# Deep cross network, last layer: the first half of the batch computed in the transposed form

## The chip, the cores and the metric

The kernel runs on one core of one Trainium2 chip. Its time is the device time of one execution in microseconds; where several runs were made, their median is given. A profile is one execution taken by the hardware profiler. TensorE is called PE, VectorE DVE, ScalarE ACT, GpSimd POOL, and SP is the engine whose queue issues most of the DMAs.

## The reference

Six cross layers over a batch of 4096 rows with 416 features, in bf16. Each layer multiplies the running value by a 416 x 416 matrix, adds a bias, multiplies by the input elementwise and adds the running value:

```python
B, F, D, L = 4096, 26, 16, 6
Din = min(F * D, 1024)          # 416

def reference(x0, ws, bs):
    x = x0
    for l in range(ws.shape[0]):
        x = x0 * (x @ ws[l] + bs[l]) + x
    return x
```

## The kernel before

**Two forms.** In the transposed form features lie on the partitions and batch rows along the free dimension. The 416 features are three blocks of 128 (`XM[..]`, index `m` or `k`) and a remainder of 32. The batch is two halves `s` of 2048 rows, each of four groups `g` of 512; the remainders of the four groups of a half are stacked on the 128 partitions of `XR`. Layers one to five (indices 0 to 4) are computed in this form. In the row form batch rows lie on the partitions, 128 at a time, and the 416 features along the free dimension; the sixth layer (index 5, `LL`) is computed in this form, so that its result can be stored to the output as it stands.

**Layers two to five** (loop at line 282). For each tile `(s, m)`, PE runs `mm_full` (line 181: per group twelve matmuls, whose weights are 32 columns wide, four of them side by side) and `mm_row` (line 187: the 32 remainder features, four groups side by side) into two PSUM tiles of 128 x 1024. `ew_main` then takes each of the two: ACT evicts it with the bias (line 165), DVE multiplies by the input (166) and adds the running value (169). `rem_pair` computes the 32 remainder outputs of both halves of the batch (`mm_rem`, lines 193 and 198; `ew_rem`, lines 173 to 175). In the order of the code each tile's elementwise work follows its matmuls, and the two tiles of a turn are interleaved.

**What the row form needs.** Besides the weights, it needs the input in rows (`X0rows`, loaded by four DMAs at line 125) and the fifth layer's result in rows (`XLrows`). The latter comes from DMA transposes on the SP queue: while layer five runs (`feeds_last`), `xl_dmat` (line 205) transposes each finished tile of 128 features x 2048 rows into `XLrows`, and the remainder goes through `scrR` (line 274) and an ACT copy `xl_rem` (line 278).

**Layer six** (from line 315). A quad is four row tiles of 128 rows that share one block of the stacked remainders; there are eight, four in each half of the batch. `mm_q_full` (line 327) is three matmuls over 416 columns per row tile; `mm_q_rem` adds the remainder features (333) and the bias (336) of four row tiles. Quads are done in rounds of two that fill the four PSUM tiles; `PAIRS`, `TURNS` and `ENDS` say which PSUM place each row tile has, and whether two are evicted together. `ew` evicts one or two row tiles by ACT (354), multiplies by `X0rows` on DVE (355), and leaves the add of `XLrows` (344) and the store (345) to `close_sum` of the next call, so that an add runs behind the next product. All stores are issued on the SP queue but the last, which is on ACT's.

**What sets the order.** The code is written for a framework that finds the waits between engines. Each engine and each DMA queue executes in one order, which follows the order of the code; `keep_in_program_order` fixes it for an instruction. PSUM has four tiles of two banks (`bufs=4`, tag `ps`) for all of this; row results lie in ten buffers `o`.

Of the kernel before, what the change touches and what calls it, by code (L numbers as in the profile page):

```python
# [10 lines left out]
ALU = mybir.AluOpType  # L11
BF16 = mybir.dt.bfloat16
FP32 = mybir.dt.float32
# [3 lines left out]
def kernel(  # L17
# [7 lines left out]
    nc = tc.nc  # L25
    B, D = x0.shape
    L = ws.shape[0]
    P = 128
# [3 lines left out]
    NS = 2  # L32
    NG = 4
    CW = 512
    SW = NG * CW
    NBT = B // P
# [3 lines left out]
    big = ctx.enter_context(tc.tile_pool(name="big", bufs=1))  # L40
    tpool = ctx.enter_context(tc.tile_pool(name="tpool", bufs=6))
    opool = ctx.enter_context(tc.tile_pool(name="opool", bufs=10))
    psum = ctx.enter_context(tc.tile_pool(name="psum", bufs=4, space=bass.MemoryType.PSUM))

    x0_v = x0.rearrange("(bt p) d -> p bt d", p=P)
    out_v = out.rearrange("(bt p) d -> p bt d", p=P)
# [9 lines left out]
    bLr = const.tile([P, D], BF16)  # L56
    bM = const.tile([P, NK, L], FP32)
    bR = const.tile([P, L], FP32)
    X0rows = big.tile([P, NBT, D], BF16)
    XLrows = big.tile([P, NBT, D], BF16)  # L60
    scrR = [big.tile([P, 4, P], BF16, name=f"scrR{s}") for s in range(NS)]
    xrem = big.tile([P, 16, R], BF16)
# [2 lines left out]
    XM = [big.tile([P, NK, B], BF16, name=f"XM{i}") for i in range(3)]  # L65
    XR = [big.tile([P, NS * CW], BF16, name=f"XR{i}") for i in range(3)]

    def col0(s, g):
        return SW * s + CW * g

    def load_wm(eng, l):
        eng.dma_start(WM[:, l], ws[l, 0:NK * P, :].rearrange("(k p) n -> p k n", p=P))
# [48 lines left out]
        load_wr(nc.sync, g, 1, L)  # L121
    for l in range(2, L):
        load_wm(nc.sync, l)
    for q in range(4):
        nc.sync.dma_start(X0rows[:, 8 * q:8 * q + 8, :], x0_v[:, 8 * q:8 * q + 8, :])
    for g in range(NG):
        nc.sync.dma_start(bLr[32 * g:32 * g + 1, :], bs[LL:LL + 1, :])

# [33 lines left out]
    def ew_main(l, s, m, h, pt, cur, nxt, pin=False):  # L162
        c0 = col0(s, 2 * h)
        t = tpool.tile([P, 2 * CW], BF16, name="t")
        nc.scalar.activation(t[:], pt[:].rearrange("p a b -> p (a b)"), ACT.Identity, bias=bM[:, m, l:l + 1], scale=1.0)  # L165
        prod = nc.vector.tensor_tensor(out=t[:], in0=t[:], in1=XM[0][:, m, c0:c0 + 2 * CW], op=ALU.mult)  # L166
        if pin:
            tc.keep_in_program_order(prod)
        nc.vector.tensor_tensor(out=nxt[:, m, c0:c0 + 2 * CW], in0=t[:], in1=cur[:, m, c0:c0 + 2 * CW], op=ALU.add)  # L169
# [7 lines left out]
    def mm_full(l, s, m, g, pts, cur, first, last):  # L177
        c0 = col0(s, g)
        for k in range(NK):
            for q in range(4):  # L180
                nc.tensor.matmul(pts[g // 2][32 * q:32 * q + 32, g % 2, :], lhsT=WM[:, l, k, 128 * m + 32 * q:128 * m + 32 * q + 32],  # L181
                                 rhs=cur[:, k, c0:c0 + CW], start=(first and k == 0), stop=(last and k == NK - 1),
                                 tile_position=(0, 32 * q))

    def mm_row(l, s, m, pts, curR, first, last):
        for g in range(NG):
            nc.tensor.matmul(pts[g // 2][:, g % 2, :], lhsT=WR[32 * g:32 * g + 32, l, 128 * m:128 * m + 128],  # L187
                             rhs=curR[32 * g:32 * g + 32, CW * s:CW * s + CW],
                             start=first, stop=last, tile_position=(32 * g, 0))
# [11 lines left out]
    def new_pts():  # L201
        return [psum.tile([P, 2, CW], FP32, tag="ps", name=f"pt{h}") for h in range(2)]

    def xl_dmat(s, k, nxt):
        nc.sync.dma_start_transpose(out=XLrows[:, 16 * s:16 * s + 16, 128 * k:128 * k + 128],
                                    in_=nxt[:, k, SW * s:SW * s + SW])
# [57 lines left out]
    for s in range(NS):  # L264
        first_layer(s)

    def rem_pair(l, cur, curR, nxtR, feeds_last):
        pr2 = psum.tile([P, 2, CW], FP32, tag="ps", name="pr2")
        for s in range(NS):
            mm_rem(l, s, pr2[:, s, :], cur, curR)  # L270
        for s in range(NS):
            ew_rem(l, s, pr2[:, s, :], curR, nxtR)
            if feeds_last:
                nc.sync.dma_start_transpose(out=scrR[s][:], in_=nxtR[:, CW * s:CW * s + CW])

    def xl_rem(s):
        tc.keep_in_program_order(
            nc.scalar.copy(XLrows[:, 16 * s:16 * s + 16, NK * P:D].rearrange("p (g i) r -> p i g r", g=NG),
                           scrR[s][:].rearrange("p i (g r) -> p i g r", g=NG)))

    cur, curR = XM[1], XR[1]
    for l in range(1, LL):
        nxt, nxtR = XM[1 + (l % 2)], XR[1 + (l % 2)]
        feeds_last = (l == LL - 1)
        tiles = [(s, m) for s in range(NS) for m in range(NK)]
        pts = {}

        def finish(t):
            s, m = t
            for h in range(2):  # L290
                ew_main(l, s, m, h, pts[t][h], cur, nxt)
            if feeds_last:
                xl_dmat(s, m, nxt)

        for n in range(0, len(tiles), 2):
            ta, tb = tiles[n], tiles[n + 1]
            pts[ta] = new_pts()
            for g in range(NG):
                mm_full(l, ta[0], ta[1], g, pts[ta], cur, True, False)
            mm_row(l, ta[0], ta[1], pts[ta], curR, False, True)  # L300
            pts[tb] = new_pts()
            mm_row(l, tb[0], tb[1], pts[tb], curR, True, False)
            if feeds_last and n == 4:
                xl_rem(0)
            finish(ta)
            for g in range(NG):
                mm_full(l, tb[0], tb[1], g, pts[tb], cur, False, True)
            finish(tb)
            if n == 0:
                rem_pair(l, cur, curR, nxtR, feeds_last)  # L310
        if feeds_last:
            xl_rem(1)
        cur, curR = nxt, nxtR

    l = LL
    quads = [(s, i) for s in range(NS) for i in range(4)]
    NQ = len(quads)
    KD = NK * P

    def q_cols(q, g):  # L320
        s, i = quads[q]
        c = col0(s, g) + 128 * i
        return slice(c, c + 128)

    def mm_q_full(q, g, py, closes):
        for k in range(NK):
            nc.tensor.matmul(py[:, 0:D], lhsT=cur[:, k, q_cols(q, g)], rhs=WM[:, l, k, :],  # L327
                             start=((not closes) and k == 0), stop=(closes and k == NK - 1))

    def mm_q_rem(q, py, done):  # L330
        s, i = quads[q]
        for g in range(NG):
            nc.tensor.matmul(py[g][:, 0:D], lhsT=curR[32 * g:32 * g + 32, CW * s + 128 * i:CW * s + 128 * i + 128],  # L333
                             rhs=WR[32 * g:32 * g + 32, l, :], start=(g >= done), stop=False, tile_position=(32 * g, 0))
        for g in range(NG):
            nc.tensor.matmul(py[g][:, 0:D], lhsT=ones[32 * g:32 * g + 1, :],  # L336
                             rhs=bLr[32 * g:32 * g + 1, :], start=False, stop=(g < done), tile_position=(32 * g, 0))
# [9 lines left out]
    def ew(q, g0, n, src, eng):  # L347
        s, i = quads[q]
        b0 = 16 * s + 4 * g0 + i
        b = slice(b0, b0 + 4 * (n - 1) + 1, 4)  # L350
        t = tpool.tile([P, 2 * CW], BF16, name="t")
        o = opool.tile([P, 2, D], BF16, name="o")
        tv = t[:, 0:n * D].rearrange("p (a d) -> p a d", a=n)
        nc.scalar.copy(tv, src)  # L354
        tc.keep_in_program_order(nc.vector.tensor_tensor(out=tv, in0=tv, in1=X0rows[:, b, :], op=ALU.mult))  # L355
        close_sum()
        pending.append((o[:, 0:n, :], tv, XLrows[:, b, :], out_v[:, b, :], eng))

    PAIRS = [(0, 0), (0, 1), (1, 0), (1, 1), (2, 0), (2, 1), (3, 0), (3, 1)]
    TURNS = [(0, 0), (0, 1), (1, 0), (2, 0), (3, 0), (1, 1), (2, 1), (3, 1)]  # L360
    ENDS = [(0, 0), (1, 0), (2, 0), (0, 1), (3, 0), (1, 1), (2, 1), (3, 1)]
    rounds = [(0, PAIRS, 2), (2, PAIRS, 2), (4, TURNS, 2), (6, ENDS, 1)]
    for q, at, done in rounds:
        tiles = [psum.tile([P, 2, CW], FP32, tag="ps", name=f"py{n}") for n in range(4)]
        bank = [tiles[n][:, a, :] for n, a in at]

        def close(u, n):
            tl, a = at[u]
            ew(q + u // 4, u % 4, n, tiles[tl][:, a:a + n, 0:D], nc.scalar if q + 2 == NQ and u == 7 else nc.sync)

        for u in range(done):
            mm_q_full(q, u, bank[u], False)
        mm_q_rem(q, bank[0:4], done)
        close(0, done)
        mm_q_rem(q + 1, bank[4:8], 0)
        for u in range(done, 8):
            mm_q_full(q + u // 4, u % 4, bank[u], True)
            if at is not PAIRS:
                close(u, 1)
            elif u % 2:  # L380
                close(u - 1, 2)
    close_sum()


# [28 lines left out]
```

## Time and profile before

| quantity | value |
| --- | --- |
| time, median of 3 runs | 130.92 us (130.61 to 130.94) |
| span of the profiled execution | 128.9 us |
| time of the profiled execution beside its span | not given by the page |
| PE busy | 123.1 us (96%) |
| DVE busy | 107.1 us (83%) |
| ACT busy | 86.9 us (67%) |
| granted PE clock, mean | 0.998 |
| moved by DMA | 16.37 MB; HBM read 6.15 MB, written 3.41 MB |
| last layer on PE | 103.85 to 124.55 us |
| last DVE add ends | 126.32 us |

The span runs from the first to the last instruction of the profiled execution. Busy time is the time in which an engine had an instruction in work. In the page, a line such as `L181 PE MATMUL pt<-XM,WM` is a group of instructions of line 181 that read `XM` and `WM` and write `pt`; a chain is the work that ended last, followed back from the end; a timeline lists instructions by start and duration; a windows view gives busy times and the DMA traffic of chosen stretches.

### The profile page before, as it was taken

How to read it: one execution, taken by the hardware profiler on the slowest of the kernel's cores; microseconds unless marked ns; L12 is line 12 of the kernel's file. 1: busy time of each engine (PE TensorE's matmuls, PEld its weight loads, DVE VectorE, ACT ScalarE, POOL GpSimd, SP SyncE). 2: the span in 40 equal slices, each digit the busy share in tenths (PEclk: the TensorE clock that was granted, in tenths of full speed). 3: DMA queues.
4: the chain of work that ended last, by engine and by line, in shares of the span. 5: the costliest groups of instructions: out<-in, count | busy, mean ns of one | idle time of the engine just before them, and what ended most of it. 6: DMA issues, size and time to landing. Idle time of an engine off the chain costs nothing.

```text
span 128.9 us, 3973 instructions
## 1 busy us (share of the span) xinstructions
PE 123.1 (96%) x1690; PEld 54.9 (43%) x1690; DVE 107.1 (83%) x197; ACT 86.9 (67%) x99; POOL 5.9 (5%) x18
## 2 busy tenths in 40 slices
PE   6999999999999999999999999999999999999960
PEld 2343443354444444444444444444444445445420
DVE  1032979999999898989898989898989899898991
ACT  0426783987848577848668848668847896569670
POOL 4022200600000000000000000000000000000000
PEclk9999999999999999999999999999999999999999
DMA  3999999999990000000000000000297999995754
GB/s 106 237 203 217 170 158 260 247 328 333 336 299 11 5 0 8 0 0 5 0 5 0 5 0 5 0 5 0 42 166 164 123 219 178 187 323 188 231 179 139
DMA packets 42102, 16.37 MB, mean 127 GB/s; under 512 B 30906, under 2 KB 42084, under 8 KB 42084
## 3 DMA queue, kind: packets, MB, share of 16 engines
q1 hardware_dynamic: 39416, 15.56, 54.6%
q10 hardware_dynamic: 2668, 0.56, 2.3%
q8 instruction: 13, 0.21, 0.7%
q14 instruction: 5, 0.04, 0.1%
HBM read 6.15 MB, written 3.41 MB: 74 GB/s over the span
## 4 chain that ended last, share of the span: by engine, by line
PE 80%; DMA 8%; DVE 5%; issue 2%; SPq 1%; ACT 1%; DVEq 0%
PE pt L181 49%; PE ph L214 9%; DMA XM<-in_x_dram 8%; PE py L327 8%; PE pt L187 5%; PE pr L198 5%; DVE t L355 3%; DVE o L344 2%; PE pr L193 2%; SPq L76 1%; PE py L333 1%; PE ph L221 1%; PE py L336 1%; ACT t L354 1%; PE pr L157 0%
## 5 line engine op out<-in xcount | busy, mean ns | idle before, releaser
L181 PE MATMUL pt<-XM,WM 128*32 128x512 bf16 x1152 | 65.2, 379 | 0.0
L165 ACT ACTIVATE t<-pt,bM 128x1024 bf16<-128x1024 f32 x48 | 49.6, 1115 | 18.3 <-PE pt L187 18.3
L166 DVE TENSOR_TENSOR t<-t,XM 128x1024 bf16<-128x1024 bf16 x60 | 41.4, 690 | 5.3 <-ACT t L165 5.3
L169 DVE TENSOR_TENSOR XM<-t,XM 128x1024 bf16<-128x1024 bf16 x60 | 41.8, 696 | 3.4
L181 PEld LDWEIGHTS <-WM 128*32 128x32 bf16 x1152 | 29.7, 97 | 33.8 <-issue 5.1
L354 ACT CAST t<-py 128x416 bf16<-128x416 f32 (+1 forms) x23 | 14.8, 642 | 4.8 <-PE py L327 2.1
L327 PE MATMUL py<-WM,XM 128*128 128x416 bf16 x96 | 17.7, 340 | 0.0
L214 PE MATMUL ph<-XM,WM 128*128 128x512 bf16 x72 | 16.5, 379 | 0.1
L165 ACT ACTIVATE t<-ph,bM 128x1024 bf16<-128x1024 f32 x12 | 12.5, 1114 | 4.4 <-PE ph L221 4.4
L327 PEld LDWEIGHTS <-XM 128*128 128x128 bf16 x96 | 9.0, 98 | 8.5 <-issue 1.4
L355 DVE TENSOR_TENSOR t<-t,X0rows 128x416 bf16<-128x416 bf16 (+1 forms) x23 | 10.4, 454 | 1.2 <-ACT t L354 1.2
L214 PEld LDWEIGHTS <-WM 128*128 128x128 bf16 x72 | 6.8, 98 | 8.6 <-issue 1.3
L344 DVE TENSOR_TENSOR o<-t,XLrows 128x416 bf16<-128x416 bf16 (+1 forms) x23 | 10.3, 451 | 0.0
L173 ACT ACTIVATE t<-pr,bR 128x512 bf16<-128x512 f32 x10 | 6.4, 684 | 2.7 <-PE pr L198 2.1
L198 PE MATMUL pr<-XM,WM 128*32 128x512 bf16 x120 | 8.2, 379 | 0.0
L187 PE MATMUL pt<-XR,WR 32*128 32x512 bf16 x96 | 7.3, 379 | 0.0
L141 PE MATMUL wps<-warm 128*128 128x512 bf16 (+1 forms) x11 | 4.4, 593 | 1.2 <-DVE warm L94 1.2
L175 DVE TENSOR_TENSOR XR<-t,XR 128x512 bf16<-128x512 bf16 x10 | 4.2, 423 | 0.7
L198 PEld LDWEIGHTS <-WM 128*32 128x32 bf16 x120 | 3.2, 97 | 3.1
L106 ACT ACT_TABLE_LOAD x1 | 1.3, 1283 | 4.3 <-DMA WM<-in_ws_dram 4.3
L174 DVE TENSOR_TENSOR t<-t,XR 128x512 bf16<-128x512 bf16 x10 | 4.2, 418 | 0.0
L152 DVE CAST bM<-pb 128x18 f32<-128x18 bf16 x1 | 0.2, 177 | 4.6 <-PE pb L151 4.6
(39 smaller groups left out, 33.6 us busy)
## 6 DMA issues: line engine op xcount, KB each, us to landing
X0rows<-in_x_dram SPq DMA_DIRECT2D x4, 832.0 KB, 11.6
out_dram<-o SPq DMA_DIRECT2D x9, 208.0 KB, 2.4
WM<-in_ws_dram SPq DMA_DIRECT2D x5, 312.0 KB
out_dram<-o SPq DMA_DIRECT2D x13, 104.0 KB, 1.7
WR<-in_ws_dram SPq DMA_DIRECT2D x4, 130.0 KB, 4.1
WM<-in_ws_dram ACTq DMA_DIRECT2D x1, 312.0 KB
XM<-in_x_dram SPq DMA_TRANSPOSE x8, 4.9
xrig<-in_x_dram ACTq DMA_DIRECT2D x4, 32.0 KB, 4.1
```

Of the source, the lines that this page charges most:

```text
L165: nc.scalar.activation(t[:], pt[:].rearrange("p a b -> p (a b)"), ACT.Identity, bias=bM[:, m, l:l + 1], scale=1.0)
L166: prod = nc.vector.tensor_tensor(out=t[:], in0=t[:], in1=XM[0][:, m, c0:c0 + 2 * CW], op=ALU.mult)
L169: nc.vector.tensor_tensor(out=nxt[:, m, c0:c0 + 2 * CW], in0=t[:], in1=cur[:, m, c0:c0 + 2 * CW], op=ALU.add)
L173: nc.scalar.activation(tr[:, 0:CW], pr, ACT.Identity, bias=bR[:, l:l + 1], scale=1.0)
L181: nc.tensor.matmul(pts[g // 2][32 * q:32 * q + 32, g % 2, :], lhsT=WM[:, l, k, 128 * m + 32 * q:128 * m + 32 * q + 32], rhs=cur[:, k, c0:c ...
L187: nc.tensor.matmul(pts[g // 2][:, g % 2, :], lhsT=WR[32 * g:32 * g + 32, l, 128 * m:128 * m + 128], rhs=curR[32 * g:32 * g + 32, CW * s:CW ...
L198: nc.tensor.matmul(pr[32 * g:32 * g + 32, :], lhsT=WM[:, l, k, NK * P:D], rhs=cur[:, k, c0:c0 + CW], start=False, stop=(k == NK - 1), tile ...
L214: nc.tensor.matmul(pt[:, gl, :], lhsT=WM[:, 0, k, 128 * m:128 * m + 128], rhs=cur[:, k, c0:c0 + CW], start=(k == 0 and not after_row), sto ...
L327: nc.tensor.matmul(py[:, 0:D], lhsT=cur[:, k, q_cols(q, g)], rhs=WM[:, l, k, :], start=((not closes) and k == 0), stop=(closes and k == NK ...
L344: tc.keep_in_program_order(nc.vector.tensor_tensor(out=o, in0=t, in1=xl, op=ALU.add))
L354: nc.scalar.copy(tv, src)
L355: tc.keep_in_program_order(nc.vector.tensor_tensor(out=tv, in0=tv, in1=X0rows[:, b, :], op=ALU.mult))
```

## The change

The last layer's first half of the batch (rows 0 to 2047) is computed in the transposed form, as layers two to five are: three tiles `(0, m)` and the remainder. Its result goes to `XM` and `XR`, is transposed by DMA into the first half of `XLrows` (three transposes, one remainder transpose into `scrR[0]`, one ACT copy) and is stored from there by four DMAs of four row tiles each on the SP queue. They stand in the code between the single row tiles of quads 5 and 6. The second half stays in the row form: quad 4 alone in pairs, quads 5 and 6 in a round of two, quad 7 alone. The fifth layer's result is transposed for the second half only, and `X0rows` holds and loads the second half only.

```diff
-    X0rows = big.tile([P, NBT, D], BF16)
+    X0rows = big.tile([P, NBT // 2, D], BF16)
...
-    for q in range(4):
-        nc.sync.dma_start(X0rows[:, 8 * q:8 * q + 8, :], x0_v[:, 8 * q:8 * q + 8, :])
+    for q in range(2):
+        nc.sync.dma_start(X0rows[:, 8 * q:8 * q + 8, :], x0_v[:, 16 + 8 * q:16 + 8 * q + 8, :])
...
-    def rem_pair(l, cur, curR, nxtR, feeds_last):
+    def rem_pair(l, halves, cur, curR, nxtR, to_rows):
         pr2 = psum.tile([P, 2, CW], FP32, tag="ps", name="pr2")
-        for s in range(NS):
+        for s in halves:
             mm_rem(l, s, pr2[:, s, :], cur, curR)
-        for s in range(NS):
+        for s in halves:
             ew_rem(l, s, pr2[:, s, :], curR, nxtR)
-            if feeds_last:
+            if s == to_rows:
                 nc.sync.dma_start_transpose(out=scrR[s][:], in_=nxtR[:, CW * s:CW * s + CW])
...
-            if feeds_last:
+            if feeds_last and s == 1:
                 xl_dmat(s, m, nxt)
...
-            if feeds_last and n == 4:
-                xl_rem(0)
             finish(ta)
...
-                rem_pair(l, cur, curR, nxtR, feeds_last)
+                rem_pair(l, range(NS), cur, curR, nxtR, 1 if feeds_last else None)
...
-    rounds = [(0, PAIRS, 2), (2, PAIRS, 2), (4, TURNS, 2), (6, ENDS, 1)]
-    for q, at, done in rounds:
-        tiles = [psum.tile([P, 2, CW], FP32, tag="ps", name=f"py{n}") for n in range(4)]
+    out_t, out_tR = XM[1 + (l % 2)], XR[1 + (l % 2)]
+
+    def finish_t(m, pts):
+        for h in range(2):
+            ew_main(l, 0, m, h, pts[h], cur, out_t)
+        xl_dmat(0, m, out_t)
+
+    def store_rows(n):
+        nc.sync.dma_start(out_v[:, 4 * n:4 * n + 4, :], XLrows[:, 4 * n:4 * n + 4, :])
+
+    p0 = new_pts()
+    for g in range(NG):
+        mm_full(l, 0, 0, g, p0, cur, True, False)
+    mm_row(l, 0, 0, p0, curR, False, True)
+    p1 = new_pts()
+    mm_row(l, 0, 1, p1, curR, True, False)
+    finish_t(0, p0)
+    for g in range(NG):
+        mm_full(l, 0, 1, g, p1, cur, False, True)
+    finish_t(1, p1)
+    rem_pair(l, [0], cur, curR, out_tR, 0)
+    p2 = new_pts()
+    for g in range(NG):
+        mm_full(l, 0, 2, g, p2, cur, True, False)
+    mm_row(l, 0, 2, p2, curR, False, True)
+
+    def new_bank(n):
+        return [psum.tile([P, 2, CW], FP32, tag="ps", name=f"py{i}") for i in range(n)]
+
+    t4 = new_bank(2)
+    bank = [t4[u // 2][:, u % 2, :] for u in range(4)]
+    mm_q_rem(4, bank, 0)
+    finish_t(2, p2)
+    for u in range(4):
+        mm_q_full(4, u, bank[u], True)
+        if u % 2:
+            ew(4, u - 1, 2, t4[u // 2][:, :, 0:D], nc.sync)
+    xl_rem(0)
+
+    rounds = [(5, TURNS, 2, 2), (7, [(0, 0), (1, 0), (0, 1), (1, 1)], 1, 1)]
+    for q, at, done, nq in rounds:
+        tiles = new_bank(2 * nq)
...
+        last = q + nq == NQ
...
-        mm_q_rem(q + 1, bank[4:8], 0)
-        for u in range(done, 8):
+        if nq == 2:
+            mm_q_rem(q + 1, bank[4:8], 0)
+        for u in range(done, 4 * nq):
             mm_q_full(q + u // 4, u % 4, bank[u], True)
-            if at is not PAIRS:
-                close(u, 1)
-            elif u % 2:
-                close(u - 1, 2)
+            close(u, 1)
+            if not last and u < 6:
+                store_rows(u - 2)
     close_sum()
```

More of the change, by code (lines that the diff above doesn't have):

```diff
@@ L354, in ew @@
         nc.scalar.copy(tv, src)
-        tc.keep_in_program_order(nc.vector.tensor_tensor(out=tv, in0=tv, in1=X0rows[:, b, :], op=ALU.mult))
+        tc.keep_in_program_order(nc.vector.tensor_tensor(out=tv, in0=tv, in1=X0rows[:, slice(b.start - 16, b.stop - 16, b.step), :], op=ALU.mult))
         close_sum()
@@ L361 @@
     ENDS = [(0, 0), (1, 0), (2, 0), (0, 1), (3, 0), (1, 1), (2, 1), (3, 1)]
-    rounds = [(0, PAIRS, 2), (2, PAIRS, 2), (4, TURNS, 2), (6, ENDS, 1)]
-    for q, at, done in rounds:
-        tiles = [psum.tile([P, 2, CW], FP32, tag="ps", name=f"py{n}") for n in range(4)]
+    out_t, out_tR = XM[1 + (l % 2)], XR[1 + (l % 2)]
[34 more added lines that the diff above has]
+        tiles = new_bank(2 * nq)
         bank = [tiles[n][:, a, :] for n, a in at]
+        last = q + nq == NQ
         def close(u, n):
             tl, a = at[u]
-            ew(q + u // 4, u % 4, n, tiles[tl][:, a:a + n, 0:D], nc.scalar if q + 2 == NQ and u == 7 else nc.sync)
+            ew(q + u // 4, u % 4, n, tiles[tl][:, a:a + n, 0:D], nc.scalar if last and u == 3 else nc.sync)
         for u in range(done):
```

## The prediction

> **What bounds the kernel now.** I read the page first, then the chain in order of time, then the timelines of DVE, ACT and the SP queue from 84 us on, and last the windows view for what the DMA engines can move. Page, engines and the slices of DMA:
>
> ```profile
> PE 123.1 (96%) x1690; PEld 54.9 (43%) x1690; DVE 107.1 (83%) x197; ACT 86.9 (67%) x99; POOL 5.9 (5%) x18
> ...
> DMA  3999999999990000000000000000297999995754
> GB/s 106 237 203 217 170 158 260 247 328 333 336 299 11 5 0 8 0 0 5 0 5 0 5 0 5 0 5 0 42 166 164 123 219 178 187 323 188 231 179 139
> ```
>
> PE is the bound up to the last layer. The DMA engines idle in the middle and are nearly full from slice 29 on (92 us): there they carry the transposes into XLrows and then the stores. The chain (start us, us, what) gives PE's prices in both forms:
>
> ```profile
> 100.60 0.54 PE pt L187 x8
> 101.14 2.70 PE pt L181 x48
> 103.85 1.16 PE py L327 x6
> 105.01 0.29 PE py L333 x4
> 105.30 0.18 PE py L336 x4
> 105.47 0.18 PE py L333 x4
> 105.65 0.18 PE py L336 x4
> 105.83 4.33 PE py L327 x24
> ...
> 126.04 0.29 DVEq L408
> ```
>
> PE starts the last layer at 103.85 and, as the timeline of PE has it, ends at 124.55; DVE's last add ends at 126.32. DVE's timeline (start us, us, operation) gives the spacing from one start to the next:
>
> ```profile
> 97.61 0.69 DVE L166 TENSOR_TENSOR t<-t,XM 128x1024 bf16<-128x1024 bf16 x1
> 98.33 0.69 DVE L169 TENSOR_TENSOR XM<-t,XM 128x1024 bf16<-128x1024 bf16 x1
> ...
> 109.07 0.58 DVE L355 TENSOR_TENSOR t<-t,X0rows 128x832 bf16<-128x832 bf16 x1
> 109.58 0.58 DVE L344 TENSOR_TENSOR o<-t,XLrows 128x832 bf16<-128x832 bf16 x1
> ...
> 123.10 0.37 DVE L355 TENSOR_TENSOR t<-t,X0rows 128x416 bf16<-128x416 bf16 x1
> 123.39 0.37 DVE L344 TENSOR_TENSOR o<-t,XLrows 128x416 bf16<-128x416 bf16 x1
> ```
>
> In the same timeline products of 1024-wide halves start at 90.12, 91.52, 92.84 and 94.24, so a half costs 1.37 us, 1.40 where the steps are 0.61 and 0.79, which I take; a pair of row tiles costs two starts of 0.50; a single row tile 0.57. The SP queue's and ACT's timelines show what the change moves:
>
> ```profile
> 97.52 2.53 SPq L274 DMA_TRANSPOSE scrR<-XR  x2
> 100.14 11.40 SPq L205 DMA_TRANSPOSE XLrows<-XM  x4
> 111.64 14.76 SPq L345 DMA_DIRECT2D out_dram<-o  x22
> ```
> ```profile
> 100.02 0.62 ACT L278 COPY XLrows<-scrR 128x512 bf16<-128x512 bf16 x1 [0.76 <-DMA scrR<-XR]
> ```
>
> A transpose holds the SP queue 2.85 us on average (11.40 for four), a remainder transpose 1.2, and the first store waits behind the last of them. The remainder issued at 97.52 let ACT go at 100.02: 2.5 us. The windows view (stretch, busy time of PE, PEld, DVE, ACT, POOL, clock, DMA share, GB/s) tells the limit of moving rows of 416 values, in loads (33 to 36) and in stores with a backlog (113 to 116), and how the run ends:
>
> ```profile
> 33.00:36.00 3.00, 3.00 (x60) 1.50 (x56) 2.93 (x6) 2.25 (x3) 0.00 (x0) 1.00 1.10 333
> 113.00:116.00 3.00, 3.00 (x30) 1.40 (x27) 2.94 (x6) 1.93 (x4) 0.00 (x0) 1.00 1.04 329
> 127.50:128.00 0.50, 0.00 (x0) 0.00 (x0) 0.00 (x0) 0.00 (x0) 0.00 (x0) 1.00 0.24 75
> 128.00:128.90 0.90, 0.00 (x0) 0.00 (x0) 0.00 (x0) 0.00 (x0) 0.00 (x0) 0.78 0.00 0
> ```
>
> Full DMA engines move 0.333 MB per us. At 75 GB/s half a microsecond holds 0.12 us of full work, so the last bytes go at about 127.7, 1.2 us ahead of the span's end. The page gives no time for the profiled execution beside its span of 128.9; the median of the three timed runs, 130.92, lies 2.0 above it, and I add 2.0 to every span below.
>
> **The change, part by part.** *PE, first half.* Rows: half of 103.85 to 124.55, 10.35 us. Transposed: three tiles of 48 full matmuls at 2.59 to 2.70, rows of 0.54 for the first two together and 0.27 for the third, and one remainder of 0.22 + 0.65 (the rows of L193 and L198 in the chain): 2.59 + 0.54 + 2.70 + 0.87 + 2.59 + 0.27 = 9.56. PE gains 0.8 us. Then quad 4 alone: 0.47 for remainder and bias, 12 x 0.18 = 2.17; PE reaches 116.05.
>
> *DVE, first half.* In before DVE runs layer five's products until 107.65, 3.8 us behind PE, and it will again. Rows cost 8 pairs x 1.01 = 8.1 us. Transposed: four halves x 1.40 from 107.95 (ACT's first eviction, 1.1 us from 106.8) to 113.55, the remainder 0.95 (two ops, 0.52 apart, and 0.43 to the next) to 114.5, two halves x 1.40 to 117.3. That is 9.35, 1.2 us more. In the second half three pairs and ten singles (3.0 + 5.7 = 8.7) stand against one pair and fourteen singles (1.0 + 8.0 = 9.0): 0.3 less.
>
> *Loads.* Two of four X0rows loads go, 1.7 MB at around 30 us. PE is unbroken in the chain from 12 us on and waits for none of them: nothing. The bound is 0 on both sides, since the cover is PE's own work of the first layers.
>
> *Layer five.* The first half's three transposes, its remainder transpose and its ACT copy (0.62, after 0.76 of waiting) go. ACT's next eviction waited for PE anyway (0.33 idle before 100.97): nothing on the path. SP is then free when the second half's tiles come, at about 101.8, 104.9 and 107.65, and at 2.85 each is done at 110.5.
>
> *SP queue, new.* Result tiles are ready at 110.75, 113.55, 114.5 (remainder) and 117.3. Issue: first 110.75 to 113.6, second to 116.4, remainder to 117.6, third to 120.5. So the remainder lands at 116.4 + 2.5 = 118.9. The shortest transposes (1.81 us in the view of line 205) would give 117.9, the longest (3.67) about 121.
>
> *ACT, a new wait.* The copy of the remainder into XLrows is held in order behind quad 4's two evictions (over at 117.2), so ACT waits from 117.2 to 118.9 and copies until 119.5. Behind it stand all evictions of quads 5 to 7; before them DVE has only quad 4's products and one add, until 118.8. Quad 5's pair: eviction 0.85 to 120.35, product to 120.85, quad 4's late add to 121.35, the next product to 121.65, the pair's add to 122.15. PE goes on meanwhile, as the four PSUM tiles of quads 5 and 6 were emptied by 117.2. DVE's rest: five more singles x 0.57 plus four, and one add, ends at about 127.5, 1.2 us later than before.
>
> *Stores, the term that decides.* Before, stores began at 111.64. Now quad 4's first must follow the third transpose, at 120.5, and the four stores of the row buffer (0.426 MB each) are queued on SP between the singles, the first behind quad 5's pair at 122.15; the third transpose has landed by then (issue to landing some 3.5 us for the one issued at 91.63, whose bytes end at 95.2). Left to move then: 4 x 0.426 + 0.213 + ten singles x 0.1065 = 2.98 MB, 8.95 us at 0.333. SP needs some 0.35 to 0.7 us per issue and so keeps the engines full. Bytes start 0.55 after the issue (the last store, issued at 126.35, is moving by 127), at 122.7, and end at 131.65. With 1.2 behind them the span is 132.85: 134.9 with the 2.0. Bounds: had the stores been back to back from 119.1 (the third transpose issued at 117.3 and the shortest), the 3.41 MB written (the page's sum for HBM) take 10.2 us, to 129.4, 132.6 in all; with two more stalls of the kind below, 137.7.
>
> The Trainium skill, "DMA: Bandwidth & Descriptors", section "Bandwidth", has larger transfers faster, 425 GB/s at 16 MB against 341 at 1 MB. The rows here say no such thing (332 GB/s over seven microseconds of loads of 832 KB), and by the page's best figure the estimate would be 7.0 us for the 2.98 MB, so 133.0, which is still slower than before.
>
> **Rivals.** *More stalls in the transposes* (slower yet). In before the transposes moved at 42 GB/s from 96 to 97 and at 25 from 103 to 104: each such hole costs some 1.4 us. My 2.85 holds an average of them; two more in the four transposes at 110 to 121 delay ACT and every store by 2.8: 137.7.
>
> *Only the ACT wait counts.* If the stores kept up, the end would follow DVE: 127.5 + 2.6 (126.32 to 128.9) + 2.0 = 132.1. Against it: they would need 2.98 MB in 5.5 us, 0.54 MB per us, which no window shows.
>
> *The rate is higher.* If the large stores ran a quarter faster than any window shows, 0.42 MB per us, 7.1 us would do: 133.0. Against it: loads of 0.832 MB and stores of 0.213 MB run alike, 333 and 329.
>
> *Not slower.* PE's 0.8 us comes through: 130.1. It needs stores that drain beside the rest until 127.7, so 10.2 us of full engines from 117.4 on, or 0.39 MB per us from 119. Row products exist at 118.8 at the earliest and the third transpose at 117.3; it decides there, and only if stores do not queue behind transposes. That the change does nothing is no case: it moves 3.4 MB of stores behind 117 us.
>
> **How the numbers follow.** Forecast as summed, 134.9: 0.65. More stalls, 137.7: 0.17. Higher rate, 133.0: 0.08. Only the ACT wait, 132.1: 0.06. Not slower, 130.1: 0.04. The range 132.3 to 137.8 takes the forecast with its bounds and the two cases beside it. A difference of 0.3% is about what this kernel's times can tell from none (130.61 to 130.94): faster 0.03, within 0.01, slower 0.96.
>
> **What would show it.** ACT idle some 1.7 us before the copy from scrR at 118 to 119, released by the DMA; DVE idle with it; PE at about 116 after quad 4; the first store from o not before 119; the DMA share near 1 and around 330 GB/s from 123 to 131, while PE and DVE are done by 128. I am wrong if the stores run well over 333 GB/s, if SP issues stores ahead of the third transpose, or if ACT does not wait.

## The result, and the profile after

The changed kernel takes 137.27 us (136.88 to 137.59), the kernel before 130.93 us beside it: a ratio of 1.048, 95% interval 1.046 to 1.051. It is slower by 6.3 us. The forecast was 134.9 in a range of 132.3 to 137.8.

The page of the profiled execution, whose span is 135.3 us (1.97 below the median, where before it was 2.0):

```profile
PE 122.6 (91%) x1780; PEld 54.3 (40%) x1782; DVE 107.5 (79%) x191; ACT 85.9 (63%) x96; POOL 5.6 (4%) x18
...
DMA  4999999999000000000000000000105999997994
GB/s 107 209 212 214 160 150 277 281 330 314 10 0 0 5 2 5 0 5 0 5 0 5 0 5 0 5 0 5 31 8 99 173 136 225 191 127 232 331 332 149
```

PE and DVE are as busy as before, within half a microsecond. What is new stands at the right end of the DMA rows: two slices above 330 GB/s just ahead of the last one, where before the last four showed 139 to 231. The queue of SP (start us, us, operation) tells what fills them:

```profile
116.27 1.52 SPq L274 DMA_TRANSPOSE scrR<-XR  x1
117.89 3.11 SPq L205 DMA_TRANSPOSE XLrows<-XM  x1
121.09 0.54 SPq L343 DMA_DIRECT2D out_dram<-o  x1
122.77 0.40 SPq L368 DMA_DIRECT2D out_dram<-XLrows  x1
123.27 0.46 SPq L343 DMA_DIRECT2D out_dram<-o  x1
123.78 0.74 SPq L368 DMA_DIRECT2D out_dram<-XLrows  x1
124.57 2.49 SPq L343 DMA_DIRECT2D out_dram<-o  x3
```

No store goes before 121.09, 9.4 us later than in the kernel before. The first row store (L368) stands ahead of quad 4's second pair (L343 at 123.27), which is not the order of the code (the description of the kernel before has the queues follow the code; for these stores that does not hold). SP's own waits say what held the row store:

```profile
SPq L368 <- DMA XLrows<-XM: 1.0, 1, 1.0
```

The windows view (stretch, busy PE, PEld, DVE, ACT, POOL, clock, DMA share, GB/s) of the end:

```profile
120.00:121.00 1.00, 0.16 (x1) 0.10 (x1) 0.58 (x2) 1.00 (x3) 0.00 (x0) 1.00 0.27 51
...
123.00:124.00 1.00, 1.00 (x12) 0.43 (x12) 1.00 (x5) 0.51 (x2) 0.00 (x0) 1.00 0.26 87
124.00:132.50 8.50, 1.49 (x8) 0.48 (x5) 3.81 (x14) 1.64 (x4) 0.00 (x0) 0.77 1.03 330
133.00:133.80 0.80, 0.00 (x0) 0.00 (x0) 0.00 (x0) 0.00 (x0) 0.00 (x0) 0.50 0.65 214
133.80:135.30 1.50, 0.00 (x0) 0.00 (x0) 0.00 (x0) 0.00 (x0) 0.00 (x0) 0.50 0.00 0
```

From 124 to 132.5 the DMA engines are full at 330 GB/s, and for the last six microseconds neither PE nor ACT nor DVE has anything to do. ACT and DVE show the wait that was forecast, and one more:

```profile
119.02 0.62 ACT L278 COPY XLrows<-scrR 128x512 bf16<-128x512 bf16 x1 [1.60 <-DMA scrR<-XR]
```
```profile
120.42 0.59 DVE L353 TENSOR_TENSOR t<-t,X0rows 128x832 bf16<-128x832 bf16 x1 [1.21 <-ACT t L352]
...
128.23 0.38 DVE L342 TENSOR_TENSOR o<-t,XLrows 128x416 bf16<-128x416 bf16 x1 [0.79 <-DMA out_dram<-o]
```

```profile
113.60 0.34 PE L331 MATMUL py<-WR,XR 32*128 32x416 bf16 x4
...
120.84 2.27 PE L325 MATMUL py<-WM,XM 128*128 128x416 bf16 x12 [0.94 <-ACT t L352]
```

ACT waits 1.60 us for the transposed remainder, DVE 1.21 us for ACT, and PE 0.94 us for ACT; and DVE's last add waits for a result buffer whose store has not yet landed.

Two theories were tested. **S**: the stores, 3.41 MB behind 121 us, are bound by the DMA engines at some 0.333 MB per us and set the end. **A**: ACT's wait and the transposed form's work set it. Ratios below are to the kernel before, run beside each (130.6 to 131.1 us); the changed kernel's is 1.048.

### The profile page after: what moved, and what is told of

It reads as the page before. It is cut to its first block, busy times and chain, and to the rows that moved or that the text cites. A ratio compares the mean times of both kernels' runs of the same rounds, so it can differ in the third digit from the quotient of the medians.

```text
span 135.3 us, 4114 instructions
## 1 busy us (share of the span) xinstructions
PE 122.6 (91%) x1780; PEld 54.3 (40%) x1782; DVE 107.5 (79%) x191; ACT 85.9 (63%) x96; POOL 5.6 (4%) x18
## 3 DMA queue, kind: packets, MB, share of 16 engines
HBM read 4.45 MB, written 3.41 MB: 58 GB/s over the span
## 4 chain that ended last, share of the span: by engine, by line
PE 78%; DMA 7%; DVE 6%; ACTq 2%; ACT 1%; issue 1%; DVEq 0%
PE pt L181 53%; PE ph L214 10%; PE pt L187 6%; PE pr L198 5%; DMA xrig<-in_x_dram 4%; DMA out_dram<-o 3%; DVE t L353 2%; DVE o L342 2%; PE pr L193 2%; PE ph L221 1%; DVE t L166 1%; ACT t L165 1%; ACTq L81 1%; ACT t L352 1%; DVE XM L169 1%
## 5 line engine op out<-in xcount | busy, mean ns | idle before, releaser
L181 PE MATMUL pt<-XM,WM 128*32 128x512 bf16 x1296 | 73.4, 380 | 0.0
L165 ACT ACTIVATE t<-pt,bM 128x1024 bf16<-128x1024 f32 x54 | 55.8, 1114 | 22.9 <-PE pt L187 22.9
L166 DVE TENSOR_TENSOR t<-t,XM 128x1024 bf16<-128x1024 bf16 x66 | 45.9, 696 | 5.8 <-ACT t L165 5.8
L181 PEld LDWEIGHTS <-WM 128*32 128x32 bf16 x1296 | 33.6, 97 | 37.8 <-issue 5.5
L325 PE MATMUL py<-WM,XM 128*128 128x416 bf16 x48 | 9.3, 340 | 0.9 <-ACT t L352 0.9
L352 ACT CAST t<-py 128x416 bf16<-128x416 f32 (+1 forms) x13 | 7.2, 589 | 0.9 <-PE py L334 0.5
L325 PEld LDWEIGHTS <-XM 128*128 128x128 bf16 x48 | 4.4, 97 | 5.7 <-issue 2.3
L353 DVE TENSOR_TENSOR t<-t,X0rows 128x416 bf16<-128x416 bf16 (+1 forms) x13 | 5.4, 419 | 1.2 <-ACT t L352 1.2
L342 DVE TENSOR_TENSOR o<-t,XLrows 128x416 bf16<-128x416 bf16 (+1 forms) x13 | 5.5, 420 | 0.8 <-DMA out_dram<-o 0.8
L198 PEld LDWEIGHTS <-WM 128*32 128x32 bf16 x132 | 3.6, 97 | 3.3
L193 PE MATMUL pr<-XR,WD 128*32 128x512 bf16 x44 | 4.3, 381 | 0.0
```

The costliest lines, as they stand in the source:

```text
L198: nc.tensor.matmul(pr[32 * g:32 * g + 32, :], lhsT=WM[:, l, k, NK * P:D], rhs=cur[:, k, c0:c0 + CW], start=False, stop=(k == NK - 1), tile ...
L342: tc.keep_in_program_order(nc.vector.tensor_tensor(out=o, in0=t, in1=xl, op=ALU.add))
```

## The experiments

**e1 and e2: leave row stores out.**

```diff
-            if not last and u < 6:
-                store_rows(u - 2)
+            # e1: nothing        e2: only for u in (2, 4)
```

> The changed kernel without its four stores of the row buffer (1.70 MB of output are left out; all compute and all transposes stay). Theory S, the stores behind 121 us are bound by the DMA engines at 0.33 MB per us: the end falls back to DVE's last add, which stood at 128.2 for want of a buffer and would stand at about 127.5; with 2.6 of last store and 2.0 around the span 132.1, so 5.2 us less than the changed kernel's 137.3. Theory A, the wait of ACT for the transposed remainder sets the loss: about 137, no change.

> The changed kernel with two of its four stores of the row buffer (0.85 MB of output left out). Theory S: the time goes by the bytes, 0.85 MB at 0.333 MB per us is 2.6 us less, 134.7. If the order or the number of DMAs on the SP queue and not the bytes set the end, it would be nearer to one end: 137 or 132. Theory A: 137.

Measured: e1 132.67 us (ratio 1.014, 1.009 to 1.019), e2 135.17 us (1.030, 1.028 to 1.033). Four stores, two, none: 137.3, 135.2, 132.7. The time follows the bytes, by 2.1 us for the first 0.85 MB and 2.5 for the second, where S had 2.6 for the first and 2.6 for the second; why the first step falls short by 0.5 is not settled. In e1 DVE ends its last add near the forecast 127.5:

```profile
127.24 0.66 DVE L342 TENSOR_TENSOR o<-t,XLrows 128x416 bf16<-128x416 bf16 x2
```

That is 127.9; before it was 126.3. A can account for what is left, 1.4% (e7 below takes the wait away too), and not for the rest.

**e3: no remainder transpose and no copy behind it.**

```diff
+    nc.gpsimd.memset(XLrows[:, 0:16, NK * P:D], 0.0)      # early
-    rem_pair(l, [0], cur, curR, out_tR, 0)
+    rem_pair(l, [0], cur, curR, out_tR, None)
-    xl_rem(0)
```

> The changed kernel without the last layer's remainder transpose and without the ACT copy behind it (32 of 416 columns of the first half are then zeros from an early memset on POOL; stores and bytes are as before). Theory A, ACT's 1.6 us of waiting and 0.6 of copying set the loss: 2.2 us less, 135.1. Theory S: ACT and DVE gain 2.2 us, but the first row store still waits for the third transpose, which comes hardly earlier (its input is ready at 117.7), and the bytes are the same: 0.3 to 0.9 less, 136.4 to 137.0.

Measured: 137.00 us, ratio 1.045 (1.042 to 1.047). ACT's wait, which is gone in this trace, is worth some 0.3 us by the medians as long as the stores are there (0.5 by the ratios, whose intervals touch). Its SP queue:

```profile
114.14 6.87 SPq L206 DMA_TRANSPOSE XLrows<-XM  x2
121.11 0.54 SPq L344 DMA_DIRECT2D out_dram<-o  x1
122.71 0.40 SPq L369 DMA_DIRECT2D out_dram<-XLrows  x1
```

The stores go at the same times as with the wait, 121.1 and 122.7, since both still stand behind the third transpose.

**e4: the SP queue in the order of the code.**

```diff
-            eng.dma_start(dst, o)
+            pin(eng, eng.dma_start(dst, o))     # keep_in_program_order on SP
-        nc.sync.dma_start(out_v[...], XLrows[...])
+        pin(nc.sync, nc.sync.dma_start(out_v[...], XLrows[...]))
```

> The changed kernel with the SP queue's stores fixed in the order of the code: the first row store comes behind quad 5's pair, instead of ahead of quad 4's second pair as the changed kernel has it. Theory Q, the queue's order is what made the end 2.4 us later than I had summed: 134.9. Theory S: the engines are idle for 0.7 us between 122.8 and 123.5 and would be fed there with quad 4's second pair (0.21 MB, 0.64 us); all else is the same backlog: 136.6.

Measured: 136.33 us, ratio 1.041 (1.036 to 1.047). The median is 0.9 us below the changed kernel's, near what S gives for the hole at 123; the two intervals touch, so the sign of it is likely and its size is not settled. The order of the queue is a small part.

**e5: e4 without the last layer's transposes** (the first half of the row buffer zeroed early).

```diff
-        xl_dmat(0, m, out_t)
-    xl_rem(0)
+    for j in range(16):
+        nc.gpsimd.memset(XLrows[:, j, :], 0.0)            # early
```

> The changed kernel with its stores in code order (as e4, 136.33) and without any transpose in the last layer: the first half of the row buffer is zeroed early by POOL instead, so the output's first half is zeros; bytes, products and sums are the same. It shows what the transposes hold back. Theory S: quad 4's stores go at about 118.8 and 119.5, quad 5's pair at 120.3 and the row stores from there; 2.98 MB at 0.333 from 120.9 end at 129.8, span 131.2, time 133.2, so 3.1 less than e4 and still 2.1 over the kernel before. If the transposes themselves were the loss: about 131.

Measured: 134.67 us, ratio 1.027 (1.025 to 1.030), 1.7 us less than e4, where 3.1 less was expected. I had the first row store going soon after quad 5's pair at 120.3; it went later:

```profile
119.26 2.16 SPq L349 DMA_DIRECT2D out_dram<-o  x3
121.51 0.44 SPq L373 DMA_DIRECT2D out_dram<-XLrows  x1
```

Even with the transposes free, and nothing held back by them, the kernel is 2.7% slower than before, and its DMA engines are full from 122.5 to 130 (331 GB/s in that window). The transposes delay the stores; the larger part of the loss, 3.6 of 6.3 us, is left when the first half's stores merely stand behind quad 4 and quad 5's pair.

**e6: the kernel before, with its first half's stores made late.** Nothing of the transposed form is in it.

```diff
+        if q < 4:   # sums go into the row buffer in place, no store
+            pending.append((XLrows[:, b, :], tv, XLrows[:, b, :], None, None))
...
+                if at is ENDS and 1 < u < 6:
+                    pin(nc.sync, nc.sync.dma_start(out_v[:, 4 * u - 8:4 * u - 4, :],
+                                                   XLrows[:, 4 * u - 8:4 * u - 4, :]))
```

> The kernel before, with one part of the change alone: the row-form results of the first half are summed into the row buffer in place, and stored by the same four stores of four row tiles, each fixed on the SP queue behind a single row tile of quad 6 (the first behind the ninth of the second half's stores). No transposed half, no ACT wait, no more transposes than before. Theory S: the first row store goes at about 122.2; 1.70 MB and five to six singles (0.6 MB) then take 7.0 us, to 129.7; span 131.1, time 133.1, slower than before by 2.2. Theory A (ACT's wait or the transposed form's compute is the loss): 130.9, as before.

Measured: 136.40 us, ratio 1.041 (1.038 to 1.044): 5.4 us of loss with the transposes and the compute of the kernel before; DVE's last add ends at 126.64, against 126.32. This is the clearest run for S. Its 5.4 us are not a share of the changed kernel's 6.3, since its row stores go 1.2 us later than there. The size was missed by 3.3 us, and the queue and the windows tell why:

```profile
118.91 4.95 SPq L350 DMA_DIRECT2D out_dram<-o  x9
123.95 0.39 SPq L389 DMA_DIRECT2D out_dram<-XLrows  x1
...
129.30 1.49 SPq L350 DMA_DIRECT2D out_dram<-o  x2
```
```profile
121.00:124.00 3.00, 3.00 (x22) 1.67 (x19) 3.00 (x12) 2.44 (x6) 0.00 (x0) 1.00 0.57 192
125.00:131.00 6.00, 0.00 (x0) 0.00 (x0) 1.64 (x6) 0.40 (x1) 0.00 (x0) 0.75 1.03 330
131.00:132.00 1.00, 0.00 (x0) 0.00 (x0) 0.00 (x0) 0.00 (x0) 0.00 (x0) 0.50 1.00 328
132.00:134.00 2.00, 0.00 (x0) 0.00 (x0) 0.00 (x0) 0.00 (x0) 0.00 (x0) 0.50 0.02 7
```

The first row store went at 123.95 and not at 122.2; until then the engines moved 192 GB/s, as fast as DVE made row tiles, and none of that spare rate can be used later. Some 2 us also lie between the last bytes and the span's end, against 1.2 in the kernel before; why is left open.

**e7: e1 and e3 together**, so neither row stores nor the wait for the remainder.

> e1 (no row stores, 132.67) and e3 (no remainder transpose and no copy behind it) together: what is left of the change on the engines without ACT's wait. DVE's gap of 1.26 us at 119.3 to 120.6 goes: 1.2 to 1.5 less than e1, 131.2 to 131.5, so PE's gain of 0.8 us does not come through, since DVE, with 0.9 us more work, sets the end. If PE set it: 130.1.

Measured: 131.68 us, ratio 1.005 (1.003 to 1.007). Without its row stores and its wait the change still does not beat the kernel before: PE ends at 124.21, against 124.55, but DVE's last add at 126.23, against 126.32, so that PE's shorter first half buys nothing.

**e8: larger pieces.**

```diff
-        nc.sync.dma_start(out_v[:, 4 * n:4 * n + 4, :], XLrows[...])
+        nc.sync.dma_start(out[0:2048, :].rearrange("(p j) d -> p j d", p=P)[:, 4 * n:4 * n + 4, :], XLrows[...])
```

> The changed kernel with the four row stores written so that one partition's four rows lie side by side in the output (3328 bytes in one piece instead of four of 832; the first half's rows are permuted by it). Same bytes. If the DMA engines are bound by bytes: 137.3, no change. If the limit is a cost per piece: the 1.70 MB go faster than 0.333 MB per us, at 0.42 by 1.1 us, 136.2.

Measured: 136.57 us, ratio 1.042 (1.037 to 1.047), on the verge of a difference. The windows in which row stores alone move show a rate that no window of a microsecond with 832-byte rows reached (at most 348 GB/s, from 115 to 116 in the kernel before):

```profile
124.00:125.00 1.00, 1.00 (x6) 0.44 (x5) 1.00 (x4) 0.73 (x3) 0.00 (x0) 1.00 1.03 393
128.50:129.00 0.50, 0.00 (x0) 0.00 (x0) 0.00 (x0) 0.00 (x0) 0.00 (x0) 0.50 1.02 399
```

So 0.333 MB per us is the engines' rate for pieces of 832 bytes, and pieces of 3328 go at 0.39 to 0.40. The Trainium skill, "Perfetto Trace Analysis", section "DMA Optimizations", says that small DMAs, below 2 KB, have a significant overhead per transfer. Read for the pieces of a DMA, the trace agrees: the rate rose by a fifth here. Half of the bytes in larger pieces are 0.8 us less at these rates, near the 0.7 us between the medians, whose ratios' intervals overlap.

**e9 and e12: the transposed half ahead.** Both compute layer six's transposed tiles ahead of layer five's last tile `(1, 2)`, so that the row buffer is full earlier; e12 keeps the SP queue in the order of the code besides.

```diff
+    two(T5(0, 0), T5(0, 1)); rem_pair(LL - 1, range(NS), cur, curR, nxtR, 1)
+    two(T5(0, 2), T5(1, 0))
+    two(T5(1, 1), T6(0)); rem_pair(LL, [0], nxt, nxtR, out_tR, 0)
+    two(T6(1), T6(2))
+    two(T5(1, 2), None); xl_rem(1); xl_rem(0)
```

> The changed kernel with its transposed half put ahead: PE's order is layer five (0,0) (0,1), both remainders, (0,2) (1,0), (1,1), then layer six transposed (0,0), remainder, (0,1), (0,2), and layer five's (1,2) last; the row stores stand in the code ahead of quad 4's. Nothing is left out. Theory S: the third transpose's input is ready one tile earlier (114.5 for 117.7) and the row stores go at about 118, so that no backlog is left behind 126; the price is PE and DVE waiting for layer five's last tile ahead of quad 4, 2 us on DVE: DVE ends at 128.3 and the time is 132.9, 4.4 less than the changed kernel. If the bytes behind 121 were not the cause, 137 or more, the wait on top.

Measured: 138.71 us, ratio 1.061 (1.058 to 1.064), slower than the changed kernel, where I had expected 132.9. DVE says why (e9):

```profile
125.34 0.59 DVE L387 TENSOR_TENSOR o<-t,XLrows 128x832 bf16<-128x832 bf16 x1 [5.59 <-DMA XLrows<-XM]
```

and SP's queue shows the transpose that it waited for behind a row store:

```profile
112.00 4.67 SPq L205 DMA_TRANSPOSE XLrows<-XM  x2
119.06 0.42 SPq L406 DMA_DIRECT2D out_dram<-XLrows  x1
119.58 3.81 SPq L205 DMA_TRANSPOSE XLrows<-XM  x1
```

The row store stood on SP until the first half's transposes had landed, and layer five's last transpose behind it.

> e9 with one thing changed: the SP queue keeps the code's order, so that layer five's last transpose (the second half's third block) goes ahead of the first row store and not behind it. In e9 (138.71) the row store waited on SP until 119.06 and that transpose was issued at 119.58, so DVE stood 5.6 us before quad 4's first add at 125.34. Theory B, that wait in the queue is what cost e9 its gain: the transpose goes at about 117.3 and lands at 120.8, DVE's add comes at 121 and its last at 128.7; the stores, 3.41 MB from 120.6 at 0.333, end at 130.8; time 134.2, 4.5 less than e9 and 3.1 less than the changed kernel, still slower than before. If DVE's wait came from PE's order of the tiles instead: 138.7, no change.

Measured: 136.64 us, ratio 1.045 (1.041 to 1.049): 2.1 of the 4.5 us forecast. The wait in the queue is shown, but it was not all: DVE still waits 2.44 us for that transpose, and now the twelve stores of `o` are queued behind four row stores.

```profile
119.18 3.89 SPq L411 DMA_DIRECT2D out_dram<-XLrows  x4
123.17 7.92 SPq L393 DMA_DIRECT2D out_dram<-o  x12
```
```profile
121.00:128.50 7.50, 4.68 (x31) 1.99 (x28) 6.49 (x20) 4.28 (x9) 0.00 (x0) 1.00 1.06 325
129.00:131.50 2.50, 0.00 (x0) 0.00 (x0) 1.34 (x4) 0.00 (x0) 0.00 (x0) 0.78 0.70 225
```

The engines are full from 121 to 128.5, and then only 70% busy, at 225 GB/s, although the adds run ahead of their stores: in the trace the last seven single stores of 0.1065 MB leave SP's queue 0.49 us apart (0.40 for the issue and 0.09 around it), which is 0.22 MB per us.

**e10 and e11: the kernel before with more pairs in its second half**, since e7 had pointed to DVE as what sets the end there.

```diff
-    rounds = [(0, PAIRS, 2), (2, PAIRS, 2), (4, TURNS, 2), (6, ENDS, 1)]
+    rounds = [(0, PAIRS, 2), (2, PAIRS, 2), (4, PAIRS, 2), (6, ENDS, 1)]   # e10; e11 pairs quad 6 too
```

> The kernel before with quads 4 and 5 evicted and summed in pairs as quads 0 to 3 are. If DVE sets the end of the kernel before, as e7 suggests: three pairs at 1.01 for six singles at 0.57 are 0.4 us less DVE work, 130.6. If PE sets it: no change, 131.0.

> As e10, and quad 6 in pairs too; quad 7 stays in single row tiles. If DVE sets the end: 0.8 us less DVE work in all, 130.2. If PE sets it, 131.0.

Measured: e10 131.89 us (ratio 1.008, 1.004 to 1.011), e11 132.32 us (1.014, 1.009 to 1.018); both slower, where a gain or no change had been expected. Less DVE work made no earlier end. In e11 DVE's last add ends at 127.26, against 126.32: with pairs DVE waits for ACT, and ACT for PE's second row tile, and three such waits in the second half cost more than the 0.8 us of work saved:

```profile
121.86 0.59 DVE L355 TENSOR_TENSOR t<-t,X0rows 128x832 bf16<-128x832 bf16 x1 [0.43 <-ACT t L354]
...
123.38 0.59 DVE L355 TENSOR_TENSOR t<-t,X0rows 128x832 bf16<-128x832 bf16 x1 [0.42 <-ACT t L354]
```
```profile
122.49 1.67 ACT L354 CAST t<-py 128x832 bf16<-128x832 f32 x3 [0.67 <-PE py L327]
```

The size of e10's loss is less sure: in its trace 0.65 us of delay stand already ahead of the changed lines (the remainder transposes start at 98.17, in the kernel before at 97.52). The amount of DVE's work is thus not alone in setting the end of the kernel before; the pace at which PE and ACT hand it row tiles does so with it. No version here beats the kernel before.

## Why the prediction was right, and where its sum was short

*Mechanism.* Right: the change moved the stores to the end, and the DMA engines set the end (e1, e2, e6). That the stores must follow the transposes is the smaller part of it: 1.7 us between e4 and e5, which takes ACT's wait away too. The rival "only the ACT wait counts" falls by e3, and "not slower" by the result; e7 shows why PE's gain does not come through.

*Number.* The measured 137.27 lies 0.5 us below the top of the range and nearer to the rival "more stalls" (137.7) than to the forecast (134.9). That the rival's figure is so close is luck: stalls can have at most 0.9 of the 2.4 us that were missed, as the parts below show.

*PE and DVE of the first half.* Right: PE took up quad 4 at 113.60 (103.85 + 9.56 = 113.41 by the sum), and the third tile was ready on DVE at 117.70 (forecast 117.3).

*SP queue and ACT's wait.* Right: the copy started at 119.02 after 1.60 us of waiting (118.9 after 1.7), the remainder transpose went at 116.27 (116.4), and quad 5's pair was summed at 122.3 (122.15). Wrong was that PE goes on meanwhile: it stood 0.94 us for ACT's evictions.

*Stores.* Right in kind, short in size: the span is 135.3 and not 132.85, so 2.4 us more. These parts make it up:

- Full traffic began at about 123.6 and not at 122.7, 0.9. The first row store was issued at 122.77 and not at 122.15, as it waited for the third transpose, which landed behind a hole (51 GB/s from 120 to 121 above; the "more stalls" rival in part), and its bytes came 0.8 us after the issue and not 0.55.
- Quad 4's second pair, 0.213 MB, was to have been moved by then, but stood behind the first row store in the queue: 0.64.
- The last four singles left SP 0.50 us apart and did not fill the engines (302 GB/s from 132 to 133, 214 from 133 to 133.8): some 0.4. The slow start of the traffic and 330 in place of 333 GB/s up to there: some 0.2.
- The end behind the last bytes took 1.5 us, not 1.2: 0.3.

The steps that failed are the third transpose landed by 122.15, SP taking the stores in the order of the code, and engines full to the last byte. The parts are read from the trace of one execution; only the second was tested by a run: e4 gained 0.9 us where it would give 0.64, with touching intervals.

*DVE's last add.* Forecast 127.5; it ended at 128.6. The sum had no wait for any of the ten result buffers, and the last add waited 0.79 us for one. It cost nothing, as the stores ended 5 us later.

*Rate.* 330 GB/s over 8.5 us against 333 assumed. The rival of a higher rate needed larger pieces, as e8 has it, and the kernel does not have them.

## What to carry to other kernels

Before work is moved to a form whose result leaves the chip later, add up the bytes that then remain, divide by the rate that the profile shows for such pieces, and compare with the compute that is left to hide them; here 3.2 MB at 0.33 MB per us, 9.6 us, met about 4 us of compute. A gain on the busiest engine (PE's 0.8 us) is worth nothing where the tail behind it is set by another engine. On a queue that issues in order, ask for each transfer that waits what stands behind it, and read the queue's real order from the trace, as it need not be the code's.

## What was not expected of the hardware

- Rows of 832 bytes moved at 325 to 333 GB/s over backlogs of three microseconds and more, loads and stores alike; pieces of 3328 bytes moved at 393 to 399 GB/s in e8.
- Transposes paused. From 120 to 121 us the engines moved 51 GB/s although a transpose was under way, and such holes stand in the kernel before too (42 GB/s from 96 to 97, 25 from 103 to 104). In the traces each comes within some 2 us of a 16 KB transfer of the instruction queues (at 118.90 in the changed kernel, 95.71 and 102.19 in the kernel before). Plain stores showed no such hole beside the one at 121.26 in e12 (325 GB/s from 121 to 128.5). That the one causes the other was not tested.
- Single stores of 0.1065 MB whose sums were ready left SP 0.49 us apart, 0.22 MB per us, which is below the 330 that the engines moved elsewhere (e12; the changed kernel's last four likewise).
